# One drain on GpSimd's queue, recorded behind the part for overflowing rows, in a strided-attention and mixture-of-experts kernel

## The chip, the core and the metric

The kernel runs on one core of a Trainium2 chip. The metric is the device time of one execution in microseconds (us). Three runs of the kernel before are given by their median, and one more execution was recorded by the profiler; every row below is from that one.

The engines are TensorE (PE; PEld is its loading of weights), VectorE (DVE), ScalarE (ACT), GpSimd (POOL) and SyncE (SP). Each has a queue of instructions of its own; a row with a q behind the engine's name (POOLq, SPq) is an instruction that the queue itself carries out: a wait on a semaphore, a branch, a drain.

## The reference

Attention first: 8 batches, 8 heads, 576 positions, 64 features per head, in float32. Four heads see the last 32 positions, four see every 32nd position. The result, 4608 rows of 512, goes through a mixture of experts: each row goes to the one expert of 8 with the highest logit, through two layers (512 to 1024, relu, 1024 to 512), and is scaled by the gate's probability and by a sigmoid.

```python
logits = x @ w_gate
e_idx = np.argmax(logits, axis=1)
gate_w = probs[np.arange(N), e_idx]
eom = 1.0 / (1.0 + np.exp(-(x @ w_output_gate)))
for e in range(E):
    mask = e_idx == e
    h = np.maximum(x[mask] @ w1[e], 0.0)
    out[mask] = gate_w[mask, None] * eom[mask, e, None] * (h @ w2[e])
```

## The kernel before

The attention fills the first third. It writes its rows to a table in device memory (xd), and counts on the way which rows go to which expert.

The experts follow (experts, L1353), one after the other in the order of their number of rows, r = 0 to 7. Each has a fixed capacity of rows (736 down to 512), worked on in blocks of up to 128 rows. For an expert, GpSimd gathers the rows of each block from xd with an indirect DMA (gather, L1032, by way of fetch, L156); TensorE turns them; layer 1 goes over eight blocks of hidden features (layer1, L1080, j = 0 to 7); layer 2 goes over the blocks of rows (layer2, L1186), the incomplete last block first (by_tail, L1145). Each block's result is scaled by ScalarE into a tile ys and sent to its rows of the output by an indirect DMA that GpSimd issues (store, L1199, the DMA on L1206). There are four tiles ys in turn. For the last block of all, VectorE scales one half. While expert r is in layer 2, the rows and weights of expert r + 1 are made ready; the last expert has no next one, so that GpSimd has nothing to gather then.

All of this is recorded under a schedule by hand (L1423): each engine gets its instructions in the order in which the Python program records them, and the waits between engines come from the tiles that they share. Whether less than a full matmul is enough, because an expert has fewer rows than its capacity, is decided at run time by branches on TensorE's queue (choose, L1258).

beyond (L1274), the part for overflowing rows, is recorded in layer 1 of the last expert, behind j = 0. It loads a number, total, into a register of every engine (L1275): the count of blocks of rows that went beyond the capacities. It has two branches on total > 0, at L1277 and at L1286; the second holds a loop. With these inputs total is 0 and both are skipped. On the skipped way an engine makes up for the semaphores that the branch would have counted up: with EVENT_SEMAPHORE, and on GpSimd's queue also with INC_SWDGE_SEM for the DMAs that it would have issued.

Behind the last expert the program ends. Its closing is on the line of the kernel's enclosing block (L1505): SyncE waits for every DMA that is still out, each engine drains its queue, all meet at a barrier, GpSimd clears the semaphores, and all meet again.

Of the kernel before, what the change touches and what calls it, by code (L numbers as in the profile page):

```python
# [59 lines left out]
def attn_moe_kernel(  # L60
# [19 lines left out]
    nc = tc.nc  # L80
# [80 lines left out]
    def load_w(r, which, eng=nc.sync, cs=range(4), raw=None):  # L161
        src = (w1 if which == 1 else w2)[bass.ds(expert(r, eng), 1)]
        for c in cs:
            raw = raw_p.tile([128, 1024], F32, name="raw") if raw is None or len(cs) > 1 else raw
            if which == 1:
                eng.dma_start(out=raw, in_=src[:, 128 * c:128 * (c + 1), :].rearrange("o p f -> p (o f)"))
            else:
                eng.dma_start(out=raw.rearrange("p (c f) -> p c f", c=2),
                              in_=src[:, 256 * c:256 * (c + 1), :].rearrange("o (c p) f -> p (o c) f", p=128))
            raws[r, which, c] = raw  # L170
# [780 lines left out]
    def rank():  # L951
        nc.vector.scalar_tensor_tensor(out=rk[:, 0, :], in0=cnt, scalar=float(E), in1=wts,
                                       op0=ALU.mult, op1=ALU.add)
        nc.vector.scalar_tensor_tensor(out=rk[:, 0, :], in0=first, scalar=65536.0, in1=rk[:, 0, :],
                                       op0=ALU.mult, op1=ALU.add)
        nc.vector.tensor_tensor(out=sq[:, 0], in0=inner(rk[:, 0, :]), in1=outer(rk[:, 0, :]), op=ALU.is_gt)
        nc.vector.tensor_reduce(out=rk[:, 1, :], in_=sq[:, 0], axis=AX.X, op=ALU.add)
        nc.vector.tensor_tensor(out=sq[:, 0], in0=inner(rk[:, 1, :]), in1=outer(eidx), op=ALU.is_equal)
        nc.vector.tensor_tensor(out=sq[:, 1], in0=sq[:, 0], in1=inner(eidx), op=ALU.mult)
        nc.vector.tensor_reduce(out=rk[:, 2, :], in_=sq[:, 1], axis=AX.X, op=ALU.add)  # L960
        nc.vector.tensor_copy(out=erank, in_=rk[:, 2, :])

    def gates():
        n = EH // 128
        nc.vector.tensor_tensor(out=gate, in0=book[:, 4], in1=book[:, 3], op=ALU.add)
        nc.vector.tensor_tensor(out=gate, in0=gate, in1=book[:, 2], op=ALU.add)
        nc.vector.tensor_tensor(out=own[:, 0, 0:n], in0=gate[:, :, 0:n].rearrange("p e k -> p k e"),
                                in1=first.unsqueeze(1).to_broadcast([128, n, E]), op=ALU.mult)
        nc.vector.tensor_reduce(out=lead_gate, in_=own[:, 0, 0:n], axis=AX.X, op=ALU.add)
# [35 lines left out]
    def blocks(r):  # L1005
        n = rows_of(r)
        return [(c, min(128, n - 128 * c)) for c in range((n + 127) // 128)]
# [24 lines left out]
    def gather(r):  # L1032
        for c, m in blocks(r):
            xg = xg_p.tile([128, DM], F32, name="xg")
            k = at_col(r, c)
            fetch(xg[0:m, :], xd[:, :], idx[0:m, r, k:k + 1] if r else idx0[0:m, k:k + 1], N)
            xgs[r, c] = xg

    def split_w(r, which, c):
        raw = raws[r, which, c]  # L1040
        if which == 1:
            split(w1h[:, c, :], w1l[:, c, :], raw)
        else:
            sl = slice(2 * c, 2 * c + 2)
            split(w2h[:, sl, :].rearrange("p c f -> p (c f)"), w2l[:, sl, :].rearrange("p c f -> p (c f)"), raw)
# [83 lines left out]
    def by_token(i, o, m, w, row, between={}, lag=0, two=False):  # L1129
        yp = rotate(yps)  # L1130
        tokens_in(yp, i, o, m, between, lag)
        return lambda: store(yp, w, row, m, two=two)
# [86 lines left out]
    def limits():  # L1219
        for r in range(E):  # L1220
            nc.gpsimd.iota(limi[:, r, :], pattern=[[128, OVR]], base=caps[r], channel_multiplier=0)
            nc.vector.memset(capf[:, r:r + 1], float(caps[r]))
# [19 lines left out]
    def count_spare():  # L1242
        nc.vector.tensor_tensor(out=sq[:, 1], in0=sq[:, 0], in1=inner(cnt), op=ALU.mult)
        nc.vector.tensor_reduce(out=held, in_=sq[:, 1], axis=AX.X, op=ALU.add)
        nc.vector.tensor_tensor(out=held, in0=ecst[:, 5, :], in1=held, op=ALU.subtract)
        nc.vector.tensor_scalar(out=held, in0=held, scalar1=0.0, scalar2=127.0, op0=ALU.max, op1=ALU.min)
        nc.vector.tensor_copy(out=spare, in_=held)
# [3 lines left out]
    def first_spare():  # L1251
        f = moe.tile([128, 2 + E], F32, name="first_spare")
        nc.vector.tensor_tensor(out=f[:, 2:], in0=cnt, in1=first, op=ALU.mult)
        nc.vector.tensor_reduce(out=f[:, 0:1], in_=f[:, 2:], axis=AX.X, op=ALU.add)
        nc.vector.tensor_tensor(out=f[:, 1:2], in0=ecst[:, 5, 0:1], in1=f[:, 0:1], op=ALU.subtract)
        nc.vector.tensor_scalar(out=spare0, in0=f[:, 1:2], scalar1=0.0, scalar2=127.0, op0=ALU.max, op1=ALU.min)
# [96 lines left out]
    def experts():  # L1353
        for c in range(4):
            load_w(0, 2, cs=[c], raw=scratch[c // 2][:, 1024 * (c % 2):1024 * (c % 2 + 1)])
        gather(0)
        for c in range(4):
            split_w(0, 2, c)
        gates()
        first_spare()  # L1360
        for hp in hps:
            nc.scalar.activation(out=hp[:, WB - STEP * (ARMS - 1):WXB], func=AF.Copy, scale=0.0,
                                 in_=ecst[:, 0, 0:1].to_broadcast([128, WXB - WB + STEP * (ARMS - 1)]))
        for c in range(2):
            split_w(0, 1, c)
        by_token(0, 0, 128, lead_gate[:, 0:1], tabe[:, 0:1], lag=2)()
        between = {j: [(turn, 0, c, m)] for j, (c, m) in zip(TURN_AT, blocks(0))}
        between[5] = [(arms, 0)]
        for c in range(2, KC):
            between[TURN_AT[c - 2]].append((split_w, 0, 1, c))  # L1370
        sent = [by_token(0, 128 * c, 128, lead_gate[:, c:c + 1], tabe[:, c:c + 1], between) for c in range(1, EH // 128)]
        hs.append(tuple(moe.tile([128, FC, WHB], F32R, name=n) for n in ("hhb", "hlb")))
        for fn in sent:
            fn()
        for r in range(E):
            nxt = r + 1 < E
            if r == 0:
                rank()
                by_rank()
            if nxt:  # L1380
                gather(r + 1)
            if r == 0:
                again = [ah_p.tile([128, 2048], F32, name=n) for n in ("hha", "hla")]
                for c in range(4):
                    load_w(0, 2, cs=[c], raw=again[c // 2][:, 1024 * (c % 2):1024 * (c % 2 + 1)])
            if r == 1:
                hs[0] = tuple(ah_p.tile([128, FC, EH], F32R, name=n) for n in ("hha", "hla"))
            for j in range(FC):
                layer1(r, j)
                if r == 0 and j == 1:  # L1390
                    count_spare()
                    send_away()
                if r == 0 and j == 5:
                    copied()
                if r == 2 and j == 7:
                    limits()
                if r == 4 and j == 4:
                    overflow()
                if r == E - 1 and j == 0:
                    beyond()  # L1400
                if r and j in (0, 1, 3, 5):
                    split_w(r, 2, (j + 1) // 2)
                if j == 1 and nxt:
                    load_w(r + 1, 1, nc.sync if r else nc.scalar)
            work = []
            if nxt:
                load_w(r + 1, 2, nc.sync if r else nc.scalar, cs=[0, 1])
                load_w(r + 1, 2, cs=[2, 3])
                ws = [(split_w, r + 1, 1, c) for c in range(KC)]
                ts = [(turn, r + 1, c, m) for c, m in blocks(r + 1)]  # L1410
                while ws or ts:
                    work += ts[:1] if len(ts) > len(ws) else ws[:1]
                    ts, ws = (ts[1:], ws) if len(ts) > len(ws) else (ts, ws[1:])
            items = len(work)
            total, done = len(blocks(r)) - 1, 0
            for p, _ in enumerate(layer2(r)):
                n = min(len(work), items * (p + 1) // total - done)
                done += n
                for fn, *a in work[:n]:
                    fn(*a)  # L1420
                work = work[n:]
# [87 lines left out]
```

## Time and profile before

| what | us |
|---|---|
| median of three runs | 610.65 (609.48 to 613.14) |
| the profiled execution, device time | 613.63 |
| its span, from the first to the last instruction | 611.8 |
| TensorE busy in it | 580.2 |
| GpSimd busy in it | 195.5 |

The rows further down come from the profile's page and from questions to the trace. Starts are in us from the start of the span. A view of one line of code lists the operations of that line by engine, with their count, their shortest, median and longest time in ns, and when the first and the last of them started. A timeline row gives the start, the duration, and in square brackets how long the engine had been idle and what ended that.

### The profile page before, as it was taken

The numbers are of one execution on the slowest core, as the hardware profiler recorded it, in microseconds if no ns is written. First come the engines' busy times: TensorE is split into PE (matmuls) and PEld (weight loads), VectorE is DVE, ScalarE is ACT, GpSimd is POOL, SyncE is SP. The second block draws the span as 40 slices with busy tenths as digits, with TensorE's granted clock in tenths as the row PEclk, the third lists the DMA queues.
The fourth block names the chain that finished last, engine by engine and source line by source line (L and its number), as shares of the span: only waits on it lengthen the run. The fifth ranks groups of instructions, "written<-read, shape, count | busy, mean of one in ns | idle before, by whom it ended". The sixth has DMA issues, their size and how long they took to land. (4 is left out here: it accounts for less than half of the span.)

```text
span 611.8 us, 14516 instructions
## 1 busy us (share of the span) xinstructions
PE 580.2 (95%) x5670; PEld 490.3 (80%) x5670; DVE 314.0 (51%) x707; ACT 278.3 (45%) x553; POOL 195.5 (32%) x275
## 2 busy tenths in 40 slices
PE   8798999989989999999999999999999999999992
PEld 6676777767768989988998899889988878877972
DVE  4886889898699453432343234324532533542510
ACT  3886777767344353333333333334243443442410
POOL 4326666686222234021401140214023123111021
PEclk9998999999999999999999999999999999999997
DMA  9998988995524845054405330543064164161000
GB/s 316 321 310 258 296 273 278 299 316 179 188 69 138 309 152 161 2 196 136 123 2 196 135 118 3 187 154 96 29 210 142 56 225 134 58 224 52 3 25 34
DMA packets 42488, 97.93 MB, mean 160 GB/s; under 512 B 5458, under 2 KB 16346, under 8 KB 42394
## 3 DMA queue, kind: packets, MB, share of 16 engines
q1 hardware_dynamic: 34122, 73.47, 37.0%
q0 software_dynamic: 6864, 19.74, 9.7%
q10 hardware_dynamic: 1408, 3.38, 1.6%
q8 instruction: 71, 1.16, 0.8%
q14 instruction: 23, 0.19, 0.1%
HBM read 77.74 MB, written 20.58 MB: 161 GB/s over the span
## 5 line engine op out<-in xcount | busy, mean ns | idle before, releaser
L1076 PE MATMUL hp<-xh,w1h 128*128 128x256 f32 (+8 forms) x384 | 127.1, 331 | 1.1 <-ACTq L1286 1.1
L1076 PE MATMUL hp<-xl,w1h 128*128 128x256 f32 (+8 forms) x384 | 126.9, 330 | 0.1
L1076 PE MATMUL hp<-xh,w1l 128*128 128x256 f32 (+8 forms) x384 | 126.8, 330 | 0.0
L1114 PE MATMUL yp<-w2h,hhb 128*128 128x512 f32 (+1 forms) x208 | 83.2, 400 | 0.0
L1114 PE MATMUL yp<-w2l,hhb 128*128 128x512 f32 (+1 forms) x208 | 81.3, 391 | 0.0
L1114 PE MATMUL yp<-w2h,hlb 128*128 128x512 f32 (+1 forms) x208 | 81.1, 390 | 0.0
L1076 PEld LDWEIGHTS hp<-xh,w1h 128*128 128x128 f32 x384 | 72.6, 189 | 4.8 <-ACTq L1286 1.4
L1206 POOL DMA_INDIRECT out_dram<-ys,idx x32 | 32.9, 1027 | 133.0 <-ACT ys L1203 128.2
L1076 PEld LDWEIGHTS hp<-xl,w1h 128*128 128x128 f32 x384 | 72.6, 189 | 3.4 <-DVE xl L994 0.4
L1076 PEld LDWEIGHTS hp<-xh,w1l 128*128 128x128 f32 x384 | 72.6, 189 | 2.8
L1206 POOL DMA_INDIRECT out_dram<-ys,ri x18 | 20.3, 1128 | 169.8 <-ACT ys L1203 166.8
L994 DVE TENSOR_TENSOR xl<-tp,xh 128x512 fp32r<-128x512 f32 (+3 forms) x40 | 25.8, 650 | 85.1 <-ACT xh L993 85.1
L993 ACT CAST xh<-tp 128x512 fp32r<-128x512 f32 (+3 forms) x40 | 22.0, 556 | 99.2 <-PE tp L1053 99.2
L1099 DVE SCALAR_TENSOR_TENSOR hlb<-hp,hhb 128x384 fp32r<-128x384 f32 (+3 forms) x48 | 28.2, 591 | 67.3 <-ACT hf L1098 67.3
L1096 ACT ACTIVATE hhb<-hp 128x384 fp32r<-128x384 f32 (+3 forms) x48 | 24.9, 518 | 79.5 <-PE hp L1076 74.3
L308 POOL TENSOR_TENSOR p_t<-p_t,st 128x512 f32<-128x512 f32 x40 | 42.6, 1065 | 54.4 <-DVE st L293 12.3
L157 POOL DMA_INDIRECT xg<-xd,idx x40 | 43.6, 1091 | 23.9 <-DVE idx L452 9.9
L1114 PEld LDWEIGHTS yp<-w2l,hhb 128*128 128x128 f32 (+1 forms) x208 | 38.8, 187 | 8.7
L1114 PEld LDWEIGHTS yp<-w2h,hhb 128*128 128x128 f32 (+1 forms) x208 | 38.9, 187 | 8.1 <-issue 0.4
L994 DVE TENSOR_TENSOR w1l<-raw,w1h 128x1024 fp32r<-128x1024 f32 x32 | 39.1, 1226 | 11.9 <-ACT w1h L993 11.7
L1203 ACT ACTIVATE ys<-yp,pages 128x512 f32<-128x512 f32 (+2 forms) x36 | 24.7, 687 | 45.0 <-issue 35.5
L1114 PEld LDWEIGHTS yp<-w2h,hlb 128*128 128x128 f32 (+1 forms) x208 | 38.9, 187 | 7.7
(217 smaller groups left out, 1075.8 us busy)
## 6 DMA issues: line engine op xcount, KB each, us to landing
raw<-in_moe_w_dram SPq DMA_DIRECT2D x54, 512.0 KB
vst<-in_vs_dram SPq DMA_DIRECT2D x8, 780.0 KB
vlt<-in_vl_dram SPq DMA_DIRECT2D x16, 292.5 KB
q_t<-in_ql_dram SPq DMA_DIRECT2D x8, 576.0 KB
q_t<-in_qs_dram SPq DMA_DIRECT2D x7, 650.0 KB
xd<-x_t SPq DMA_DIRECT2D x80, 54.0 KB
xd<-x_t SPq DMA_DIRECT2D x16, 256.0 KB
raw<-in_moe_w_dram ACTq DMA_DIRECT2D x6, 512.0 KB
```

The lines of the kernel that those rows point to most:

```text
L157: nc.gpsimd.indirect_dma_start(out=dst, out_offset=None, in_=src, in_offset=bass.IndirectOffsetOnAxis(ap=idx, axis=0), bounds_check=top, o ...
L308: nc.gpsimd.tensor_tensor(out=p_t, in0=p_t, in1=st, op=ALU.subtract)
L993: nc.scalar.copy(out=hi, in_=src)
L994: nc.vector.tensor_tensor(out=lo, in0=src, in1=f32(hi), op=ALU.subtract)
L1076: nc.tensor.matmul(out=hp[:, 0:n], lhsT=w[:, k, 128 * j:128 * (j + 1)], rhs=x[:, k, 0:n], start=first, stop=(k == KC - 1 and w is w1l))
L1096: nc.scalar.activation(out=hh[:, j, 0:s], in_=hp[:, 0:s], func=AF.Relu)
L1099: nc.vector.scalar_tensor_tensor(out=hl[:, j, 0:s], in0=hp[:, 0:s], scalar=0.0, in1=f32(hh[:, j, 0:s]), op0=ALU.max, op1=ALU.subtract)
L1114: nc.tensor.matmul(out=yp[0:m, :], lhsT=h[:, j, o:o + m], rhs=w[:, j, :], start=(n == 0), stop=(n == len(order) - 1))
L1203: nc.scalar.activation(out=ys[0:m, 0:h], in_=yp[0:m, 0:h], func=AF.Copy, scale=w[0:m, :])
L1206: i = nc.gpsimd.indirect_dma_start(out=out.rearrange("t (k d) -> (t k) d", k=k), out_offset=bass.IndirectOffsetOnAxis(ap=row, axis=0), in_ ...
```

## The change

One instruction is recorded behind beyond(): a drain on GpSimd's queue.

```diff
@@ -1398,6 +1398,7 @@
                     overflow()
                 if r == E - 1 and j == 0:
                     beyond()
+                    nc.gpsimd.drain()
                 if r and j in (0, 1, 3, 5):
                     split_w(r, 2, (j + 1) // 2)
                 if j == 1 and nxt:
```

In the code it stands behind both branches of beyond, not within them, and it names no tile.

## Rows read from the trace of the kernel before

**Rows 1.** The page's head and its list of engines.
```profile
span 611.8 us, 14516 instructions
PE 580.2 (95%) x5670; PEld 490.3 (80%) x5670; DVE 314.0 (51%) x707; ACT 278.3 (45%) x553; POOL 195.5 (32%) x275
```

**Rows 2.** Stretches of the end: each engine's busy time, clock, DMA share.
```profile
core 0: us, PE busy (x) PEld busy (x) DVE busy (x) ACT busy (x) POOL busy (x), PEclk, DMA share, GB/s
...
563.60:580.70 17.10, 17.10 (x86) 15.80 (x88) 9.47 (x11) 8.13 (x16) 0.00 (x0) 1.00 0.01 4
...
605.60:611.00 5.40, 0.00 (x0) 0.00 (x0) 0.00 (x0) 0.00 (x0) 0.00 (x0) 0.50 0.00 0
```

**Rows 3.** Line L1505, the closing: GpSimd's drains, SyncE's from 600 on, VectorE's last.
```profile
L1505 POOLq DRAIN  x3: 46/109/9037, 602.0 to 611.6; - x3
...
L1505 SPq EVENT_SEMAPHORE  x10: 28/28/28, 604.9 to 605.5; - x10
L1505 SPq DRAIN  x2: 7/10/13, 605.6 to 605.6; - x2
...
L1505 DVEq DRAIN  x1: 19/19/19, 611.3 to 611.3; - x1
```

**Rows 4.** Timeline: GpSimd's stores around its pause, the last matmul, scaling and store.
```profile
561.19 0.97 POOL L1206 DMA_INDIRECT out_dram<-ys,idx  x1 [4.07 <-ACT ys L1203]
585.33 0.97 POOL L1206 DMA_INDIRECT out_dram<-ys,ri  x1 [23.17 <-ACT ys L1203]
...
600.45 0.39 PE L1114 MATMUL yp<-w2l,hhb 128*128 128x512 f32 x1
601.43 0.48 DVE L1205 TENSOR_SCALAR ys<-yp,pages 128x256 f32<-128x256 f32 x1 [18.13 <-ACT ys L1203]
602.19 0.97 POOL L1206 DMA_INDIRECT out_dram<-ys,idx  x1 [4.77 <-DVE ys L1205]
```

**Rows 5.** Stores from 580 on; landing of the last, and of those from 561.2 to 596.4.
```profile
L1206 POOL DMA_INDIRECT out_dram<-ys,ri x3: 967/970/972, 585.3 to 587.9; - x3
L1206 POOL DMA_INDIRECT out_dram<-ys,idx x3: 967/970/971, 591.0 to 602.2; - x3
...
DMA to landing us min/median/max: 2.7/2.7/2.7
...
DMA to landing us min/median/max: 2.1/2.5/3.2
```

**Rows 6.** Line L1499, the program's start: GpSimd's queue.
```profile
L1499 POOLq INC_SWDGE_SEM  x1: 27/27/27, 0.1 to 0.1; - x1
L1499 POOLq DRAIN  x1: 183/183/183, 0.3 to 0.3; - x1
```

**Rows 7.** GpSimd's DMAs of the whole span, by line.
```profile
L157 POOL DMA_INDIRECT xg<-xd,idx x40 | 43.6, 1091 | 23.9 <-DVE idx L452 9.9 <-issue 8.2 <-DVE idx L981 2.5
L1206 POOL DMA_INDIRECT out_dram<-ys,idx x32 | 32.9, 1027 | 133.0 <-ACT ys L1203 128.2 <-DVE ys L1205 4.8
L1206 POOL DMA_INDIRECT out_dram<-ys,ri x18 | 20.3, 1128 | 169.8 <-ACT ys L1203 166.8 <-issue 3.1
...
L157 POOL DMA_INDIRECT xg<-xd,tabe x2 | 2.2, 1119 | 0.3 <-DMA xd<-x_t 0.2 <-issue 0.2
L1206 POOL DMA_INDIRECT out_dram<-ys,tabe x2 | 2.0, 1017 | 14.0 <-ACT ys L1203 14.0
...
L108 POOL DMA_DIRECT2D tri<-in_tri_dram x1 | 0.7, 727 | 0.0
```

**Rows 8.** Lines L1277 and L1286, the two skipped branches: GpSimd's queue.
```profile
L1277 POOLq INC_SWDGE_SEM  x1: 1980/1980/1980, 564.4 to 564.4; - x1
...
L1286 POOLq INC_SWDGE_SEM  x1: 1937/1937/1937, 566.9 to 566.9; - x1
```

**Rows 9.** Line L1206 on GpSimd's queue, from 568 to 584.
```profile
L1206 POOLq EVENT_SEMAPHORE  x4: 17/43/13218, 569.0 to 569.2; - x4
```

**Rows 10.** Timeline: TensorE's first matmul behind the skipped branches.
```profile
563.59 0.47 PE L1076 MATMUL hp<-xh,w1h 128*128 128x440 f32 x1 [1.05 <-ACTq L1286]
```

## The prediction

> **What bounds the kernel now.** I read the page's head first. TensorE is busy for 580.2 of the 611.8 us of the span, so almost any gain has to come from TensorE's time or from the ends, where TensorE has no work [rows 1]. Then I cut the end of the span into stretches. In layer 1 of the last expert (563.6 to 580.7) TensorE is busy for all of the 17.10 us and GpSimd executes nothing. From 605.6 to 611.0, behind the last store, no engine is busy and the DMA engines' share is 0.00: 5.4 us in which the chip shows no work at all [rows 2].
>
> What fills these 5.4 us is on the line of the kernel's end, L1505. GpSimd's queue has a DRAIN there that starts at 602.0 and takes 9.037 us, so it ends at 611.0 [rows 3]. The last store starts at 602.19 and takes 0.97 us on GpSimd, to 603.16 [rows 4]; it lands 2.7 us after its start, at 604.9 [rows 5]. SyncE, which waits for every DMA, agrees: it goes on at 604.9, works through ten waits and passes its own two drains at 605.6 [rows 3]. TensorE, ScalarE and VectorE are through before: the last matmul starts at 600.45, the last scaling ends at 601.9 [rows 4]. So at 605.6 four engines stand at the closing barrier, and GpSimd's drain holds it for another 5.4 us. What follows it (barrier, clearing of semaphores, second barrier) runs from 611.0 to the end of the span.
>
> **What the drain does in that time** the trace does not say outright; three rows bear on it. (1) In the first microsecond GpSimd also has a DRAIN, of 0.183 us, before any of its DMAs [rows 6], and the two that follow the long one at the end take 0.109 and 0.046 us [rows 3]. A drain of this queue is short when no DMA was issued since the last one. (2) GpSimd issues 95 DMAs in the program: 40 + 32 + 18 + 2 + 2 + 1 [rows 7]. None of its drains stands between the first of them and the long one. (3) Another instruction of this queue, INC_SWDGE_SEM, which the skipped branches of the part for overflowing rows issue, takes 27 ns before the first DMA [rows 6] but 1.980 and 1.937 us in the last expert, when 89 have been issued, all of them landed by then [rows 8]. So something about finished DMAs stays on GpSimd's books and is gone through again. I take the long drain to go through the same books, once for each DMA since the last drain, and to leave them empty.
>
> **The change, part by part.** It adds one instruction and moves or removes none; no DMA is added.
>
> The added drain. It is recorded behind the second skipped branch, so it begins when that branch's INC_SWDGE_SEM is over: 566.9 + 1.937 = 568.9 [rows 8]. The store before it was issued at 561.2 and landed 3.2 us later at the latest, at 564.4 [rows 5], when the first INC_SWDGE_SEM began [rows 8]. So the drain waits for no transfer, only for its own walk over 95 - 6 = 89 DMAs (six stores come after it [rows 5]). No row shows a price for one DMA in a drain, so I bound it. From above: the whole 9.037 us over 95 is 95 ns. From below: 1.937 us over 89 is 22 ns, the INC_SWDGE_SEM's walk. In between: counted from the landing of the last store, (611.0 - 604.9) / 95 = 64 ns; counted from the end of its issue, (611.0 - 603.16) / 95 = 82 ns. I take 64 to 82 ns, since these come from a drain. The added drain then costs 5.7 to 7.3 us (bounds 2.0 to 8.5) and ends between 574.6 and 576.2 (bounds 570.9 to 577.4).
>
> What is queued behind it on GpSimd: the four waits of the first store of the last expert. The last of these began at 569.2 and stood for 13.218 us, until 582.4 [rows 9], and the store itself started at 585.33, after 23.17 us in which GpSimd executed nothing [rows 4]. So 5.0 us of cover remain to 582.4 even at the upper bound, and 7.9 us to the store. No engine waits for GpSimd here: TensorE's first matmul behind the branches starts at 563.59 [rows 10], before GpSimd has even begun its first INC_SWDGE_SEM. On the path: 0. If the cover were gone, the stores would be late, but five of them have only to leave before the sixth at 602.19, so most of a delay would be taken up there too.
>
> The drain at the end. It now has the six stores behind the added drain to go through: 6 x 64 to 82 ns is 0.4 to 0.5 us (bounds 0.13 to 0.57), behind the landing at 604.9 at the latest. So it ends between 605.0 and 605.5. What is late next is SyncE, whose drains are passed at 605.6. That is why the price of one DMA does not matter for the sum: within its bounds GpSimd is there before SyncE. The barrier then opens at 605.7 (605.6 plus a tenth for the hand-over) where it opened at 611.0: 5.3 us less. The closing 0.8 us stay.
>
> **The sum.** Layer 1: +0. End: -5.3 us. The profiled execution takes 613.63 us, 1.8 us more than its span; it becomes 608.3. It is 2.98 us above the median of the runs, 610.65, and above the highest of them, 613.14. The saving does not hang on that difference, so I carry it to the median: 610.65 - 5.3 = **605.3 us**, 0.9% less. About 0.5% (3.05 us) is what a measurement of this kernel can tell from no change.
>
> **Rivals.** First, **the long drain is no sum over DMAs but one fixed piece of work**, due whenever any DMA was issued since the last drain: asking every DMA queue once whether it is idle, a settling time behind the last landing, or a wait for something that is no work of GpSimd's. Then the added drain pays some 6.1 us (611.0 - 604.9) in the hidden place, and the end pays them again for its six stores: 610.65, no change. For it: the short drains had no DMA at all before them [rows 3, 6], so they don't tell "few" from "many". Against it: INC_SWDGE_SEM grew from 27 ns to 1.9 us with nothing in flight [rows 6, 8], and that looks like a list. With it goes the case that the added drain does not empty the books, and the case that the 5.4 us belong to the profiled execution alone. Together 0.12.
>
> The Trainium skill (VectorE: DVE Perf Modes, section "The DRAIN you can't avoid") has a rule by which this rival would come out: the drains around a program are a constant of about 12 ns on all five engines, so that one more neither costs nor saves, and the time would be 610.65. The trace agrees for SyncE, with 7 and 13 ns, and in the last round for VectorE, with 19 ns, and disagrees for GpSimd, with 9.037 us [rows 3].
>
> Second, on the other side, **the drain ties the other engines**. It names no tile; if the recorder took it for an order over everything, as it would a barrier, TensorE's next matmuls in layer 1 would wait for its end. The place is 563.59, the price 574.6 to 576.2 minus 563.59, 11.0 to 12.6 us, with 5.3 us given back at the end: about 616.3 to 618.0, say 617. It decides as soon as any wait of TensorE ends behind 568.9, for 5.3 us are used up by then. Against it: the order of the work is written by hand here, engine by engine, waits come from tiles, and a drain has none. 0.04.
>
> Third, inside the forecast: **a part of the long drain is fixed** and only the rest a sum. If 1.5 us were fixed, the end's drain would reach to 604.9 + 1.5 + 0.5 = 606.9, and 4.1 us would be saved: 606.5.
>
> **How the numbers follow.** The forecast has 0.84, the first rival 0.12, the second 0.04. The three runs lie 1.2 us below to 2.5 us above their median, and the fixed part may cost up to 2 us or so; that makes 603.4 to 607.9 for the forecast's own range, which holds about 0.95 of its cases, so 0.80 of all. It need not reach to the rivals. Faster by over 0.5%: 0.82 (the forecast less a little for a large fixed part). Within 0.5%: 0.14. Slower: 0.04.
>
> **What would show it.** In the profile of the changed kernel there should be a DRAIN on GpSimd's queue at some 568.9, of 5.7 to 7.3 us, with the first store of the last expert still started by ScalarE and not by it; and the drain on the line of the kernel's end should fall from 9.04 us to between 3.1 and 3.6 us, its end before SyncE's. If the added drain is long and the last one still ends 6 us behind the last landing, the first rival holds. If the added drain takes under 0.5 us, the books are not what I think. If TensorE has a gap behind 563.59 that ends with GpSimd, the second holds.

## The result, and the profile after

| what | before, us | after, us |
|---|---|---|
| median of 20 runs | 611.38 (609.48 to 613.14) | 606.14 (604.3 to 611.11) |
| profiled execution, its span | 611.8 | 604.1 |

The ratio is 0.9912, with a 95% interval of 0.9898 to 0.9927: 5.2 us off the medians, where 5.3 was forecast.

First GpSimd's queue in the changed kernel, asked by line (count, shortest/median/longest ns, first and last start in us). L1401 is the added drain; the closing is L1506 now, one line further down. They answer to [rows 8, 9, 3].

```profile
L1277 POOLq INC_SWDGE_SEM  x1: 1980/1980/1980, 561.9 to 561.9; - x1
...
L1286 POOLq INC_SWDGE_SEM  x1: 1937/1937/1937, 564.4 to 564.4; - x1
...
L1401 POOLq DRAIN  x1: 7337/7337/7337, 566.4 to 566.4; - x1
...
L1206 POOLq EVENT_SEMAPHORE  x4: 17/43/5992, 573.8 to 574.0; - x4
...
L1506 POOLq DRAIN  x3: 46/109/3270, 599.5 to 603.8; - x3
...
L1506 SPq EVENT_SEMAPHORE  x10: 28/28/28, 602.5 to 603.1; - x10
L1506 SPq DRAIN  x2: 7/7/7, 603.1 to 603.2; - x2
```

Read it against the rows of before from top to bottom. The drain starts as the second INC_SWDGE_SEM ends (564.4 + 1.937) and takes 7.337 us. The wait behind it, for the first store's row numbers, began at 569.2 and stood for 13.218 us before; now it begins at 574.0 and stands for 5.992. The drain has eaten 7.2 us of a wait that was there anyway. At the end the drain falls from 9.037 to 3.270 us and is over at 599.53 + 3.270 = 602.80 (the start is from the chain of waits below). SyncE passes its own drains at 603.2, 0.4 us later: it is what the barrier waits for now.

The timeline of the changed kernel, the stores around the pause and the last one, and TensorE behind the skipped branches [rows 4, 10]; then the end of the chain of waits, and each engine's busy time while the added drain runs (columns as in [rows 2]):

```profile
558.78 0.97 POOL L1206 DMA_INDIRECT out_dram<-ys,idx  x1 [4.06 <-ACT ys L1203]
561.19 0.47 PE L1076 MATMUL hp<-xh,w1h 128*128 128x440 f32 x1 [1.06 <-ACTq L1286]
582.92 0.97 POOL L1206 DMA_INDIRECT out_dram<-ys,ri  x1 [23.18 <-ACT ys L1203]
599.76 0.97 POOL L1206 DMA_INDIRECT out_dram<-ys,idx  x1 [4.77 <-DVE ys L1205]
```

```profile
599.53 1.20 POOLq L1506
```

```profile
566.35:573.69 7.34, 7.34 (x38) 6.90 (x37) 3.75 (x5) 3.21 (x8) 0.00 (x0) 1.00 0.02 6
```

GpSimd's pause is 23.18 us (before: 23.17), and ScalarE ends it as before; TensorE's gap behind the branches is 1.06 us (before: 1.05), and for the 7.34 us of the added drain TensorE is busy throughout. From its first matmul behind the branches to the last store it is 38.57 us, and it was 38.60: nothing in layer 1 or layer 2 has moved. From the start of the last store to the end of the span it is 604.1 - 599.76 = 4.3 us, where it was 611.8 - 602.19 = 9.6: 5.3 us less.

The two spans differ by 7.7 us, though. The other 2.4 us are no work of the change: they are there before the first store of the experts. That store in three traces, before, after, and in the first experiment below, which has no drain added:

```profile
185.38 1.03 POOL L1206 DMA_INDIRECT out_dram<-ys,tabe  x1 [7.92 <-ACT ys L1203]
```

```profile
182.87 1.03 POOL L1206 DMA_INDIRECT out_dram<-ys,tabe  x1 [7.89 <-ACT ys L1203]
```

```profile
182.38 1.03 POOL L1206 DMA_INDIRECT out_dram<-ys,tabe  x1 [7.91 <-ACT ys L1203]
```

So the stretch up to this store, most of it the attention, took 2.5 to 3.0 us longer in the trace of before than in the other two, with or without a drain added; what made it longer is not known. From here on I read the end alone: last store to end of span.

### The profile page after: what moved, and what is told of

Read it like the earlier page. It is cut to its first block, busy times and chain, and to the rows that moved or that the text cites. A ratio compares the mean times of both kernels' runs of the same rounds, so it can differ in the third digit from the quotient of the medians.

```text
span 604.1 us, 14517 instructions
## 1 busy us (share of the span) xinstructions
PE 578.7 (96%) x5670; PEld 489.2 (81%) x5670; DVE 313.9 (52%) x707; ACT 278.4 (46%) x553; POOL 195.7 (32%) x275
## 5 line engine op out<-in xcount | busy, mean ns | idle before, releaser
L1206 POOL DMA_INDIRECT out_dram<-ys,idx x32 | 32.9, 1029 | 133.0 <-ACT ys L1203 128.2
L1206 POOL DMA_INDIRECT out_dram<-ys,ri x18 | 20.4, 1132 | 169.7 <-ACT ys L1203 166.7
```

Of the source, the lines that this page charges most:

```text
L1206: i = nc.gpsimd.indirect_dma_start(out=out.rearrange("t (k d) -> (t k) d", k=k), out_offset=bass.IndirectOffsetOnAxis(ap=row, axis=0), in_ ...
```

## The experiments

Theory A is the forecast's: a drain of GpSimd's queue goes through a list of the DMAs issued since the last one and empties it.

**A no-operation in the drain's place** (e1).

```diff
                     beyond()
-                    nc.gpsimd.drain()
+                    nc.gpsimd.nop()
```

> A no-operation of GpSimd's queue stands where the drain stood. Theory A (the drain goes through a list of the DMAs issued since the last drain, some 82 ns each, and empties it): nothing is emptied, the drain at the end takes 9.0 us again, ratio to the kernel before 1.000. Rival D (any instruction there helps, by a shift of the queue's code or by a new order of its waits): the drain at the end falls to about 3.3 us and the ratio is 0.991.

Ratio 1.0001 (0.9974 to 1.0027). GpSimd's closing:

```profile
L1506 POOLq DRAIN  x3: 46/109/9037, 599.1 to 608.7; - x3
```

9.037 us, to the nanosecond what it was [rows 3]. This does not put rival D out by itself: the no-operation left no row in the trace (14516 instructions, as before [rows 1], where one drain makes it 14517 and two 14518), so it may not have been there at all. What puts rival D out is e2, e3 and e9 below: neither a shift of the queue's code nor a new order of its waits would make the last drain follow the number of DMAs left for it.

**The drain in layer 1 of expert 2**, with 39 DMAs issued and 56 to come (e2).

```diff
                     beyond()
+                if r == 2 and j == 0:
                     nc.gpsimd.drain()
```

> The drain moves from the last expert to layer 1 of expert 2, where GpSimd has issued 39 of its 95 DMAs. Theory A: it takes 39 x 82 ns = 3.2 us there; the drain at the end has 56 left, 4.6 us behind the issue of the last store, so 5.8 us in all in place of 9.0; ratio 0.9947 (3.2 us less). The two INC_SWDGE_SEM, if they walk the same list, have 50 in place of 89 DMAs: 1.1 us each in place of 1.9. Rival B (one fixed piece of work, due once in a program or once after any large number of DMAs): 7.3 us in expert 2, 3.3 us at the end, ratio 0.991, INC_SWDGE_SEM still 1.9 us.

Ratio 0.996 (0.9936 to 0.9984), where 0.9947 was expected. GpSimd's queue and the last store:

```profile
L1277 POOLq INC_SWDGE_SEM  x1: 1200/1200/1200, 563.9 to 563.9; - x1
...
L1402 POOLq DRAIN  x1: 9081/9081/9081, 297.5 to 297.5; - x1
...
L1507 POOLq DRAIN  x3: 52/109/5852, 601.5 to 607.9; - x3
```

```profile
601.73 0.97 POOL L1206 DMA_INDIRECT out_dram<-ys,idx  x1 [4.77 <-DVE ys L1205]
```

The drain at the end takes 5.852 us (5.8 expected) and reaches 4.65 us behind the issue of the last store (601.5 + 5.852 - 601.73 - 0.97): 56 x 82 ns is 4.6. Last store to end of span: 608.2 - 601.73 = 6.5 us, between 9.6 and 4.3, as the list has it. A fixed piece would have given 4.3 and a ratio of 0.991: rival B is out. INC_SWDGE_SEM falls to 1.200 us with 50 DMAs on the list.

The added drain missed its number. It does not stand in a clear pause here: its row starts at 297.5, while three gathers ahead of it are still to be issued, and the last of those ends at 302.1. The drain ends at 306.6, 4.5 us later and not 3.2. In these 4.5 us the share of the DMA engines, the last but one number of a row, is this:

```profile
302.10:304.60 2.50, 2.50 (x16) 2.48 (x16) 0.56 (x1) 1.49 (x4) 0.00 (x0) 1.00 0.57 180
304.60:306.60 2.00, 2.00 (x16) 2.00 (x16) 1.94 (x4) 1.17 (x5) 0.00 (x0) 1.00 0.00 0
```

So the gathers are in flight up to 304.6, and the drain ends 2.0 us behind them, where 3.2 us from the issue would have had it end at 305.3: it waited for a gather to land, which the place in the last expert spared it.

**The drain between the last two stores** (e3), in store, for the block that is scaled in two halves alone.

```diff
+        if two:
+            nc.gpsimd.drain()
         i = nc.gpsimd.indirect_dma_start(
```

> The drain moves to the place between the last two stores, with 94 DMAs issued and no pause of GpSimd to hide it. Theory A: it takes 94 x 82 ns = 7.7 us from the end of the fifth store's issue, so the last store starts some 3 us later than before, and the drain at the end is short; of the 5.3 us only 2 to 2.5 us are left: ratio 0.996 to 0.997. Rival E (the drain's work runs beside the stores wherever it stands): ratio 0.991, last store not delayed.

Ratio 0.9978 (0.9959 to 0.9997), where 0.996 to 0.997 was expected. The added drain, and the timeline of the last two stores:

```profile
L1207 POOLq DRAIN  x1: 8960/8960/8960, 596.2 to 596.2; - x1
```

```profile
596.48 0.97 POOL L1208 DMA_INDIRECT out_dram<-ys,idx  x1 [4.47 <-ACT ys L1203]
606.07 0.97 POOL L1208 DMA_INDIRECT out_dram<-ys,idx  x1 [8.62 <-issue]
```

The last store waits 8.62 us behind the fifth in place of 4.77, so it is 3.85 us late (3 expected: the drain is over at 605.2, 7.75 us behind the fifth store's issue, but 0.9 us more go by before the store starts). The end is 610.4 - 606.07 = 4.3 us, as in the changed kernel. 5.3 won and 3.85 paid leave 1.5 us, and 1 - 1.5 / 611.9 is 0.9976. The drain is real work on GpSimd, and it was free only in the pause: rival E is out.

**Two drains in a row** (e4, one run).

```diff
                     nc.gpsimd.drain()
+                    nc.gpsimd.drain()
```

> Two drains in a row at the place of the change. Theory A: the first takes 7.3 us, the second under 0.2 us, since the list is empty; the end as with one. Rival F (a drain walks everything issued so far, and only what was issued behind the last landing is cheap at the end): the second takes 7.3 us too.

```profile
L1401 POOLq DRAIN  x1: 7337/7337/7337, 567.3 to 567.3; - x1
...
L1402 POOLq DRAIN  x1: 40/40/40, 574.7 to 574.7; - x1
```

40 ns on an empty list, and 3.275 us at the end, as with one drain: rival F is out, a drain empties the books. With these two rows the price is (7.337 - 0.040) / 89 = 82.0 ns for each DMA.

**The drain ahead of the part for overflowing rows** (e5, one run).

```diff
+                    nc.gpsimd.drain()
                     beyond()
-                    nc.gpsimd.drain()
```

> The drain is recorded ahead of the part for overflowing rows. Theory A, with INC_SWDGE_SEM walking the same list at some 22 ns per DMA: the drain still takes 89 x 82 ns = 7.3 us (or until 0.1 us behind the landing of the last store, if that is later); both INC_SWDGE_SEM fall from 1.9 us to under 0.1 us; the drain at the end takes 3.3 us. Rival G (INC_SWDGE_SEM walks something else, and its growth was no evidence): both stay at 1.9 us. TensorE should not wait for GpSimd in either case.

```profile
L1400 POOLq DRAIN  x1: 8547/8547/8547, 559.3 to 559.3; - x1
...
L1277 POOLq INC_SWDGE_SEM  x1: 189/189/189, 569.4 to 569.4; - x1
...
L1286 POOLq INC_SWDGE_SEM  x1: 146/146/146, 570.1 to 570.1; - x1
```

The drain's row is longer than the 7.3 us expected, since it begins while the store ahead of it is still being issued: that issue ends at 560.5, and the drain 7.35 us later, at 567.8. Both INC_SWDGE_SEM fall from 1.9 us, to 0.19 and 0.15 us, where I had said under 0.1. So this instruction does walk the same list, with a fixed part of its own: (1.980 - 0.189) / 89 is 20 ns per DMA, and with e2's 50 DMAs 0.189 + 50 x 0.020 is 1.19, measured 1.200. Rival G is out. TensorE's gap behind the branches is 1.06 us here too. The span is 604.8 us.

**What the price hangs on**: ten more DMAs ahead of the drain, of 8 bytes each (e6) or of 128 rows of 512 bytes (e7), one run each.

```diff
                     beyond()
+                    for i in range(10):
+                        nc.gpsimd.dma_start(out=table[i:i + 1, :], in_=slots[0:1, 0:TW])
                     nc.gpsimd.drain()
```

```diff
                     beyond()
+                    for i in range(10):
+                        nc.gpsimd.dma_start(out=xd[128 * i:128 * (i + 1), 0:128], in_=ident)
                     nc.gpsimd.drain()
```

> Ten more DMAs of 8 bytes each, to a table that nothing reads here, ahead of the added drain. If the price is per DMA: the drain takes 99 x 82 ns = 8.2 us, 0.8 us more than with 89. If it is per descriptor or per byte: the same 7.3 us within 0.2.

> Ten more DMAs of 128 rows of 512 bytes each, to rows of a table that nobody reads any more, ahead of the added drain. If the price is per DMA, whatever is in it: 8.2 us, as with ten of 8 bytes, unless the drain has to wait for the last of them to land. If it is per descriptor: 8.2 us here and 7.3 us with the tiny ones.

The last nine of the ten DMAs and the drain behind them, for e6 and then for e7:

```profile
567.53 4.53 POOL L1402 DMA_DIRECT2D table<-slots  x9
...
L1403 POOLq DRAIN  x1: 9598/9598/9598, 570.6 to 570.6; - x1
```

```profile
569.58 4.83 POOL L1402 DMA_DIRECT2D xd<-ident  x9
...
L1403 POOLq DRAIN  x1: 9822/9822/9822, 572.7 to 572.7; - x1
```

The drains' rows begin while DMAs ahead of them are still being issued. From the end of the tenth (572.06 and 574.41) to the end of the drain (580.2 and 582.5) it is 8.1 us in both, as far as the tenths of the drains' starts allow, where 0.040 + 99 x 0.082 is 8.16; with 89 it was 7.34. So ten DMAs cost some 0.8 us, whatever is in them. It is per DMA, not per row or per byte.

**A drain in layer 1 of each of the experts 1 to 7** (e8, measured twice).

```diff
                     beyond()
+                if r and j == 0:
                     nc.gpsimd.drain()
```

> A drain in layer 1 of each of the experts 1 to 7, the last of them ahead of nothing new. Theory A: each takes 82 ns for each DMA since the one before it (some 27, 12, 11, 12, 12, 10 and 5 DMAs: 2.2, 1.0, 0.9, 1.0, 1.0, 0.8 and 0.4 us, 7.3 us in all), all of it in GpSimd's pauses; the end as in the changed kernel; ratio 0.991. Rival: a piece of fixed work in each drain, which would make the sum larger than 7.3 us by seven times that piece.

> The drain in each of the experts 1 to 7 once more. If the drains in the earlier experts cost nothing on the path (their rows lie in GpSimd's pauses): the same ratio as the changed kernel of this call within 0.002. If they cost 2 us or so, as the first measurement could be read: 0.994 to 0.995.

> The changed kernel once more, beside a drain in each expert, on one chip: ratio 0.991 within 0.002.

The first measurement gave 0.9953 (0.9928 to 0.9979), 2 us or so worse than the change alone, though its end was no different. The second, beside the changed kernel on one chip, gave 0.9915 (0.9891 to 0.9939), and the changed kernel 0.9909 (0.9889 to 0.9929). So no loss can be shown, and no gain either. The seven drains of the second trace:

```profile
L1402 POOLq DRAIN  x7: 452/8463/9490, 233.3 to 562.3; - x7
```

The shortest is the last expert's, with five DMAs on the list and nothing in flight: 0.452 us is 0.040 + 5 x 0.082. The other six are long because their rows begin while gathers ahead of them are still being issued, as in e2, and so the sum was not the 7.3 us that I expected; the rival, a fixed piece in each drain, fails on the shortest row and not on the sum. From the end of the last gather's issue to the drain's end it is 2.4 to 3.9 us in these six, where 10 to 27 DMAs at 82 ns are 0.9 to 2.3 us. That made me doubt the single walk, and led to the last experiment.

**The drain in layer 1 of expert 4**, with 33 DMAs left (e9, one run).

```diff
                     beyond()
+                if r == 4 and j == 0:
                     nc.gpsimd.drain()
```

> The drain moves to layer 1 of expert 4, so that 33 DMAs are left for the end. The runs so far fit two passes over the list of 41 ns each per DMA, the second only behind the last landing. Two passes: the drain at the end is over at the later of 0.04 + 33 x 0.082 = 2.75 us behind the last store's issue and 0.04 + 33 x 0.041 = 1.4 us behind its landing; the landing comes some 1.77 us behind the issue, so 3.15 to 3.2 us behind the issue. One pass beside the transfer (the reading so far): 2.75 us behind the issue. In expert 4 the drain has 62 DMAs and waits for the last gather to land: two passes 2.6 us behind that landing, one pass sooner.

GpSimd's closing drains, then the last store; after it SyncE's wait for its landing, with its two closing drains and the one behind the barrier:

```profile
L1507 POOLq DRAIN  x3: 52/109/4374, 599.6 to 604.6; - x3
...
L1507 SPq EVENT_SEMAPHORE  x12: 17/28/28, 602.6 to 604.8; - x12
L1507 SPq DRAIN  x3: 7/7/13, 603.2 to 604.3; - x3
```

```profile
599.86 0.97 POOL L1206 DMA_INDIRECT out_dram<-ys,idx  x1 [4.77 <-DVE ys L1205]
```

The drain ends at 599.6 + 4.374 = 604.0: 3.17 us behind the issue, where one pass beside the transfer gives 2.75, and 1.4 us behind the landing at 602.6. That is what two passes of 41 ns give, the second only when everything has landed. SyncE passed its two drains from 603.2 on, so 33 DMAs left over cost 0.7 us at the barrier: from the last store to the end of the span it is 604.9 - 599.86 = 5.0 us in place of 4.3. The added drain itself, in expert 4, does not tell the two readings apart: it ended 5.1 us behind the last gather's issue, and 62 DMAs at 82 ns from there are 5.1 us.

## Why the prediction was right

**What bounds the end.** Right. The 5.4 us without any work [rows 2] were GpSimd's drain, and they went when its list was short.

**The list.** Right, and now shown: the added drain's 7.337 us with 89 DMAs, 0.452 with five, 0.040 with none lie on one line, 0.040 us + 82.0 ns for each DMA. The old end lies on it too: 0.040 + 95 x 0.082 = 7.83 us behind the end of the last store's issue at 603.16, which is 611.0. Of the two readings offered, 64 ns from the landing and 82 ns from the issue, the second was the price. The bound from INC_SWDGE_SEM, 22 ns, was another instruction's price on the same list.

**The added drain.** 7.34 us against 5.7 to 7.3, just at the upper edge, for that reason. Its cover was what was named: the first store's wait, with 6.0 us of it left.

**The end's drain.** 3.27 us against 3.1 to 3.6. That it would not hold the barrier, and that SyncE would, came out: 602.80 against 603.2. The argument given for it was a little too simple. The prediction put the walk, 0.4 to 0.5 us for six DMAs, behind the landing at the latest; half of it comes there. With six DMAs that is 0.29 us (0.040 + 6 x 0.041), and SyncE is slower than that.

**The sum.** 5.3 us on the path, 5.3 at the end of the trace, 5.2 between the medians. The forecast of 605.3 hung on the median of three runs, 610.65; with 20 runs the kernel before stands at 611.38, and that is most of the 0.8 us by which the time missed it.

**The rivals.** The fixed piece fell with e2 and e4, and with e4 the case that a drain does not empty the books. That the 5.4 us belong to the profiled execution alone fell with the 5.2 us between the medians of the runs. By the Trainium skill's 12 ns for every drain around a program (VectorE: DVE Perf Modes, section "The DRAIN you can't avoid") nothing would have changed; GpSimd's drain measures from 0.040 to 9.037 us here, so for this queue the measurement decides against carrying the figure over. That section of the Trainium skill speaks of the drains that the runtime puts before and behind a kernel; whether those on the kernel's own last line are of that kind is not shown here. That the drain ties other engines fell with TensorE's 7.34 us of work in the 7.34 us of the added drain. The third case, a fixed part of 1.5 us, is 0.040 us.

## What to carry to other kernels

A kernel that issues many DMAs from GpSimd pays for all of them in the last drain, 82 ns each here, counted from the issue of its last store; of the 7.8 us for 95 DMAs 6.1 came after that store had landed. One drain in a pause of GpSimd late in the program takes that off the end; it has to stand where the pause is longer than its walk and nothing is in flight, for it also waits for landings (e2), and between two stores it gives most of the gain back (e3). How few DMAs are left behind it matters only down to what the other engines' closing hides: six cost nothing here, 33 cost 0.7 us, and more drains than one won nothing.

## What the runs showed of the hardware that I had not expected

Half of the drain's walk, some 41 ns per DMA, comes only when the last DMA has landed: the ends lie 0.1 us behind the last landing with one DMA (e3, 608.9 against 608.8), 0.3 us with six (602.8 against 602.5) and 1.4 us with 33. Two readings of the list would do this; that there are two is my reading of these numbers and not shown. The price does not hang on a DMA's size: ten of 8 bytes and ten of 128 rows of 512 bytes both add 0.8 us. INC_SWDGE_SEM, issued for a branch that was not taken, walks the same list at 20 ns per DMA on top of 0.15 to 0.19 us; in the changed kernel it still spends 3.9 us in the two skipped branches, hidden in the same pause.
